# Attention and two gated MLPs on one core: weight sums made earlier, decoding tied to the hidden split, new homes for two kinds of tiles

## The chip, the core and the metric

The kernel runs on one core of a Trainium2 chip. The metric is the device time of one launch in microseconds (us), here of the only core. TensorE (PE) does the matmuls, VectorE (DVE), ScalarE (ACT) and GpSimd (POOL) the elementwise work, SyncE (SP) issues nearly all DMAs. Each engine works through its instructions in the order in which they stand in its own queue; between engines they wait on semaphores.

## What is computed

```python
scores = scale * q @ k.T              # B 4, H 8, S 576, D 64; causal window of 64
attn = softmax(where(mask, scores, -1e9)) @ v
x = attn.transpose(0, 2, 1, 3).reshape(2304, 512)
x = (sigmoid(x @ w_gate) * (x @ w_val)) @ w_out      # d_ff 1536
out = ((x @ w_a) * (x @ w_b)) @ w_out2               # d_ff 1536
```

q, k and v are 4-byte floats; the six weight matrices arrive as 8-byte floats. Every weight is taken apart on the chip into a high and a low 4-byte word (a pair), and a product of two pairs is three matmuls (high x high, high x low, low x high).

## The kernel before

**Weights.** The hidden width 1536 is cut into NF = 12 blocks of 128. Number F = 0 to 11 stands for a block of the first MLP, 12 to 23 for one of the second; each F has three matrices "a", "b", "o". `load_matrix` loads one with its 8-byte words into a tile `st` (three buffers). For the first MLP `first_words` (L378) makes the low word `low` on ACT (L382, a tile of its own with one buffer), |w| as `ex` on ACT (L385), the shifted high word `wi` on DVE (L391), and adds `low` to it on POOL (L395). `second_words` (L399) does it for the second MLP, on ACT (L404, L407, L408) and DVE (L413, L414, L416). `decode_pair` then writes the high word (ACT, L433) and the low word (DVE or POOL, L436), and the pair is stored to DRAM, to be fetched again later.

**Seven products.** Pairs of token blocks are multiplied by a scheme with seven products in place of eight. It wants sums of quarter matrices: `combining` (L450) makes four sums of matrix F on POOL (L457), their high words on ACT (L462, tiles `wq`), their low words on POOL (L465), and stores them as `kq` (L467). This is done for the second MLP alone. For the first MLP's second pass (the back blocks) `in_parts` (L864) makes the same sums from the fetched full weight `wf`: POOL L871, ACT L875, POOL L878. `weight_sums` (L318) makes the sums of the output matrices of five pairs p = 0 to 4: POOL L332 and L341 (`osum`), ACT L343 and DVE L344 (`opair`, one tile with one buffer, tag "op6"), one store of 1 MB each (L346, `ks`).

**Stages**, in order of time:
- 0 to 130 us: attention tiles and decoding of matrices F = 0 to 6, in an order written out by hand (`RAMP`).
- 130 to 270: the rest of the attention, the first MLP of the front blocks, decoding of F = 7 to 11. From here on the order is set by a scheduler that simulates a timeline.
- 270 to 343: `weight_sums` and the operands of the seven products (`front_operands`, ACT L766, DVE L772, L775), beside the last products of the first MLP (`gated` L501, `split_hidden` L490, `first_projection` L565).
- 343 to 548: twelve quads, the second MLP of the front blocks. A `quad` (L965) does the products 1, 5, 6, 2, 7, 4, 3 (`multiply`, L898); ACT copies three of them out of PSUM (`r`, L917), DVE adds them (L921, L931) and `split_hidden` splits the two halves of the hidden block (`hl` and `h`, ACT L494, DVE L496). Three PSUM banks `qa`, `qb`, `qc` are used per quad, from two pools in turn, so that product 2 of a quad, the first that writes `qc`, can only start when the quad before the last has been split out of the same bank. Behind each product `between(i)` may call `paced()` (L1224), which emits one step of decoding or of combining for a matrix two quads ahead, ordered behind the newest matmul and, on ACT, behind the newest copy `r`. Ordered here means: the scheduler must place it behind, with no semaphore.
- 548 to 572: operands for the back blocks (`operands` L800: ACT L812, DVE L813 and L820), `fetch` of matrix 0 and its `in_parts`.
- 572 to 937: both MLPs of the back blocks.

```python
            for _ in range(((0, 0, 0, 0, 2, 2, 2) if fc == 0 else (1, 1, 1, 0, 1, 1, 1))[i]):
                paced()
...
    ahead(0)
    next(unfinished[0])
    fill(len(rest))
```

The first two lines give, for each of the seven products of a quad, how many decoding steps go behind it; the last three fetch matrix 0 for the back blocks and begin its `in_parts`.

Of the kernel before, what the change touches and what calls it, by code (L numbers as in the profile page):

```python
# [23 lines left out]
def tile_window_attention_gated_mlps(ctx, tc, q, k, v, w1g, w1v, w1o, w2a, w2b, w2o, out):  # L24
# [273 lines left out]
    def whole(steps):  # L298
        while True:
            try:  # L300
                next(steps)
            except StopIteration as end:
                return end.value
# [14 lines left out]
    def weight_sums(p):  # L318

        both = late["hs"].tile([P, 2, DM], F32R, tag="hs", name="of").bitcast(F32)  # L320
        lows = {}
        for i in range(2):
            F = 2 * p + i
            if F < DECODED:
                lows[i] = late["rs"].tile([P, W], F32, tag="r", name="ol")
                for j, t in enumerate((both[:, i], lows[i])):
                    nc.sync.dma_start(out=t, in_=kept[F, "o"][:, j])
            else:
                nc.sync.dma_start(out=both[:, i], in_=kept_o[F])
        yield  # L330
        for i, low in lows.items():
            nc.gpsimd.tensor_tensor(out=both[:, i], in0=both[:, i], in1=low, op=ALU.add)  # L332
        (a11, a21), (a12, a22) = ((both[:, i, 0:CH], both[:, i, CH:]) for i in range(2))
        u, v = (late["sts"].tile([P, CH], F32, tag="s", name="osum") for _ in range(2))
        o = late["op6"].tile([P, 4, 2, CH], F32R, tag="op6", name="opair")
        for todo in (
            ((u, a21, a22, ALU.add, 0), (v, a11, a21, ALU.subtract, 2)),
            ((u, u, a11, ALU.subtract, 1), (v, a12, u, ALU.subtract, 3)),
        ):
            for s, x, y, op, _ in todo:  # L340
                nc.gpsimd.tensor_tensor(out=s, in0=x, in1=y, op=op)  # L341
            for s, _, _, _, n in todo:
                nc.scalar.activation(out=o[:, n, 0], in_=s, func=AF.Copy)  # L343
                nc.vector.tensor_tensor(out=o[:, n, 1], in0=s, in1=o[:, n, 0].bitcast(F32), op=ALU.subtract)  # L344
        yield
        nc.sync.dma_start(out=kept_sums[p], in_=o.bitcast(F32))  # L346

# [30 lines left out]
    def first_words(F, i, nm):  # L378
        st = staged.pop((F, nm))
        w0, w1 = st[:, :, 0], st[:, :, 1]  # L380
        low = dec.tile([P, DM], I32, tag="low", name="low")
        nc.scalar.activation(out=low, in_=w0.bitcast(U32), func=AF.Copy, scale=2.0 ** -29)  # L382
# [67 lines left out]
    def combining(F):  # L450
        got = parts[F]
        halves(got)
        (a1, a2), (b1, b2) = ((f[:, 0:CH], f[:, CH:]) for f in (full.pop((F, nm)) for nm in "ab"))
        sums = {}
# [9 lines left out]
        for n, (nm, t) in enumerate(tiles.items()):  # L464
            nc.gpsimd.tensor_tensor(out=t[:, 1], in0=sums[nm], in1=t[:, 0].bitcast(F32), op=ALU.subtract)  # L465
            got[nm] = (t[:, 0], t[:, 1])
            nc.sync.dma_start(out=kept_q[F - NF][:, n], in_=t.bitcast(F32))  # L467

    kept_q = [dram.tile([P, 4, 2, CH], F32, tag=f"kq{p}", name=f"kq{p}") for p in range(NF)]

# [205 lines left out]
    def step_decode(turn):  # L676

        if combined_by:
            parts_done[0] += 1
            if next(combined_by[0], combined_by) is combined_by:  # L680
                combined_by.pop()
                parts_done[0] = 0
                return True
            if parts_done[0] == 1:
                return True
# [155 lines left out]
    def fetch(F, whole):  # L841

        got = {}
        second = F >= NF
        for nm in "abo" if whole or second else "afbo":
# [4 lines left out]
            if nm == "a" and second and not whole:  # L850
                for n, k in enumerate(SUMS):
                    t = late["wq"].tile([P, 2, CH], F32R, tag="wq", name=f"wq{k}")
                    nc.sync.dma_start(out=t.bitcast(F32), in_=kept_q[F - NF][:, n])
                    got[k] = (t[:, 0], t[:, 1])
# [48 lines left out]

    nquad, copied = [0], []

    def products(ph, w, x, g, second):
# [16 lines left out]
        def finish(i, vv):  # L923
# [13 lines left out]
            else:  # L937
                t = second()
                t = (t[:, 0], t[:, 1])
            whole(split_hidden(ph, t, f))  # L940
            if second is None:
                nc.scalar.activation(out=g[i], in_=f, func=AF.Copy)
# [281 lines left out]
    def paced():  # L1224
# [5 lines left out]
        for i in nc.cur_bb.bb.instructions[since:]:  # L1230
            for after in (at, *(copied[-1:] if i.engine == mybir.EngineType.Activation else ())):
                if i.engine != mybir.EngineType.SP:
# [10 lines left out]
    for fc in range(NF):  # L1243
# [18 lines left out]
        extra = max(0, len(rest) - sum(counts[0]))  # L1262

        def between(i):
            fill(counts[0][i] + (extra if i == 4 else 0))
            for _ in range(((0, 0, 0, 0, 2, 2, 2) if fc == 0 else (1, 1, 1, 0, 1, 1, 1))[i]):
                paced()
# [48 lines left out]
    ahead(0)  # L1316
    next(unfinished[0])
    fill(len(rest))
    rest.extend(lambda j=j: half_projection(j) for j in range(2))
    held_back(lambda: next(unfinished[0]))  # L1320
    whole(unfinished.pop())
    SLOTS = {4: (1, 0, 1, 0, 1, 1, 0), 7: (0, 1, 1, 1, 2, 1, 1)}
# [143 lines left out]
```

## Time and profile before

| | us |
|---|---|
| median of 3 runs | 938.92 (937.58, 938.92, 942.02) |
| the profiled execution | 939.03 |
| its span on the core | 937.3 |
| PE busy | 919.2 (98%) |
| DVE busy | 671.7 (72%) |
| ACT busy | 506.3 (54%) |
| POOL busy | 296.9 (32%) |

The span is what the profiler saw of the core's instructions; 1.7 us of the profiled execution lie around it. PE's granted clock was 1.00 in every stretch. The chain of work that ended last lies on PE for 72% of the span, on DVE for 12%, ACT 6%, DMA 4%, POOL 4%; 2% are issue. An engine's idle time counts only where PE waits behind it.

### The profile page before, as it was taken

The numbers are of one execution on the slowest core, as the hardware profiler recorded it, in microseconds if no ns is written. First come the engines' busy times: TensorE is split into PE (matmuls) and PEld (weight loads), VectorE is DVE, ScalarE is ACT, GpSimd is POOL, SyncE is SP. The second block draws the span as 40 slices with busy tenths as digits, with TensorE's granted clock in tenths as the row PEclk, the third lists the DMA queues.
The fourth block names the chain that finished last, engine by engine and source line by source line (L and its number), as shares of the span: only waits on it lengthen the run. The fifth ranks groups of instructions, "written<-read, shape, count | busy, mean of one in ns | idle before, by whom it ended". The sixth has DMA issues, their size and how long they took to land.

```text
span 937.3 us, 15579 instructions
## 1 busy us (share of the span) xinstructions
PE 919.2 (98%) x5498; PEld 772.3 (82%) x5498; DVE 671.7 (72%) x1334; ACT 506.3 (54%) x1107; POOL 296.9 (32%) x325
## 2 busy tenths in 40 slices
PE   7899999999999999999999999999999999999998
PEld 6798888887888787888887887888888888888886
DVE  6997787785756778778888776688877773354455
ACT  7897555676754548785686445654544333211211
POOL 4543222332326723361653348345341000000000
PEclk9999999999999999999999999999999999999999
DMA  8988597985676824864966768454547574555212
GB/s 216 262 217 227 197 333 282 338 285 167 213 257 252 299 113 141 283 223 185 336 234 216 266 173 239 176 180 168 180 148 241 176 278 146 169 157 151 85 57 90
DMA packets 145564, 195.78 MB, mean 209 GB/s; under 512 B 63568, under 2 KB 98640, under 8 KB 144848
## 3 DMA queue, kind: packets, MB, share of 16 engines
q1 hardware_dynamic: 144400, 192.71, 62.6%
q0 software_dynamic: 1088, 2.10, 1.4%
q8 instruction: 43, 0.70, 0.3%
q14 instruction: 33, 0.27, 0.1%
HBM read 118.75 MB, written 71.57 MB: 203 GB/s over the span
## 4 chain that ended last, share of the span: by engine, by line
PE 72%; DVE 12%; ACT 6%; DMA 4%; POOL 4%; issue 2%; SPq 0%; DVEq 0%; POOLq 0%; ACTq 0%
PE qa L898 17%; PE accq L1037 12%; PE qb L898 8%; PE gps L485 7%; PE vps L485 6%; PE accm L587 6%; PE qc L898 4%; PE accy L1000 3%; PE accx L1000 2%; PE xps L231 2%; PE sps L173 1%; POOL s L457 1%; PE tps L221 1%; DMA st_b<-in_moe_w_b_dram 1%; PE acc L538 1%
## 5 line engine op out<-in xcount | busy, mean ns | idle before, releaser
L898 PE MATMUL qa<-op,wq 128*128 128x512 f32 x432 | 112.5, 390 | 1.0 <-ACT r L917 1.0
L917 ACT ACTIVATE r<-qa 128x512 f32<-128x512 f32 x108 | 62.7, 595 | 92.2 <-PE qa L898 90.9
L898 PE MATMUL qb<-op,wq 128*128 128x512 f32 x432 | 110.4, 389 | 0.0
L485 PE MATMUL vps<-xh,wb 128*128 128x256 f32 (+1 forms) x392 | 104.9, 337 | 0.8 <-ACT hr L505 0.8
L485 PE MATMUL gps<-xh,wa 128*128 128x256 f32 (+1 forms) x392 | 104.5, 337 | 0.0
L898 PEld LDWEIGHTS qa<-op,wq 128*128 128x128 f32 x432 | 81.0, 188 | 18.2 <-ACT r L917 1.4
L898 PEld LDWEIGHTS qb<-op,wq 128*128 128x128 f32 x432 | 81.1, 188 | 17.1 <-ACT op L766 0.2
L395 POOL TENSOR_TENSOR wi<-wi,low 128x512 int32<-128x512 int32 x36 | 49.4, 1373 | 127.6 <-DVE wi L391 80.6
L587 PE MATMUL accm<-hh,wo 128*128 128x512 f32 (+1 forms) x296 | 84.9, 356 | 0.4 <-ACT hh L494 0.4
L485 PEld LDWEIGHTS vps<-xh,wb 128*128 128x128 f32 x392 | 68.7, 189 | 8.7 <-ACT hr L505 1.0
L485 PEld LDWEIGHTS gps<-xh,wa 128*128 128x128 f32 x392 | 68.7, 189 | 8.2 <-DVE hl L496 0.4
L1037 PE MATMUL accq<-wo,h 128*128 128x512 f32 (+1 forms) x294 | 71.0, 385 | 0.1
L494 ACT ACTIVATE hh<-qa 128x512 fp32r<-128x512 f32 x36 | 21.4, 596 | 88.6 <-DVE qa L931 55.4
L485 PE MATMUL gps<-xl,wa 128*128 128x256 f32 (+1 forms) x196 | 65.9, 336 | 0.6 <-DVE xl L240 0.6
L485 PE MATMUL vps<-xl,wb 128*128 128x256 f32 (+1 forms) x196 | 65.7, 335 | 0.0
L1037 PEld LDWEIGHTS accq<-wo,h 128*128 128x128 f32 x294 | 54.5, 188 | 11.3 <-DVE res L1041 0.3
L878 POOL TENSOR_TENSOR wq<-s,wq 128x256 fp32r<-128x256 f32 x48 | 38.4, 868 | 76.0 <-ACT wq L875 76.0
L587 PEld LDWEIGHTS accm<-hh,wo 128*128 128x128 f32 x296 | 52.9, 189 | 9.2 <-ACT hh L494 0.6
L898 PE MATMUL qc<-op,wa 128*128 128x512 f32 x216 | 56.7, 390 | 2.4 <-DVE h L496 2.4
L192 ACT ACTIVATE pr<-pr,stat 128x128 f32<-128x128 f32 x144 | 54.1, 392 | 4.2 <-DVE stat L186 4.0
L898 PE MATMUL qa<-op,wa 128*128 128x512 f32 x216 | 56.0, 390 | 0.2 <-DVE g L921 0.2
L1037 PE MATMUL accq<-wo,hh 128*128 128x512 f32 x184 | 55.1, 391 | 0.2
(198 smaller groups left out, 2160.1 us busy)
## 6 DMA issues: line engine op xcount, KB each, us to landing
wo<-ko SPq DMA_DIRECT2D x27, 512.0 KB, 4.2
wa<-ka SPq DMA_DIRECT2D x27, 512.0 KB, 4.3
st_o<-in_moe_w_out_dram SPq DMA_DIRECT2D x24, 512.0 KB, 5.8
ka<-wa SPq DMA_DIRECT2D x24, 512.0 KB, 5.4
kb<-wb SPq DMA_DIRECT2D x24, 512.0 KB, 5.7
ko<-wo SPq DMA_DIRECT2D x24, 512.0 KB, 5.1
kq<-wq SPq DMA_DIRECT2D x48, 256.0 KB, 5.0
wq<-kq SPq DMA_DIRECT2D x48, 256.0 KB, 3.1
```

Of the source, the lines that this page charges most:

```text
L173: nc.tensor.matmul(sps[e][rows, j, :], lhsT=qt[dims, j, rows], rhs=kt[dims, j, s * WIN:s * WIN + P], start=True, stop=True,)
L192: nc.scalar.activation(out=pr[e][:, j, :], in_=pr[e][:, j, :], func=AF.Exp, bias=nmax[:, e, j:j + 1], scale=-1.0, accum_out=None if t in O ...
L231: nc.tensor.matmul(xps[dims, j, rows], lhsT=vv[:, 2 * j + e, :], rhs=pt[e][:, j, rows], start=True, stop=True)
L395: (nc.vector if F >= NF else nc.gpsimd).tensor_tensor(out=wi, in0=wi, in1=low, op=ALU.add)
L485: nc.tensor.matmul(ps, lhsT=a[:, c * P:(c + 1) * P], rhs=b[:, c, :], start=(n == 0), stop=(n == 3 * NP - 1))
L494: nc.scalar.activation(out=hh, in_=hr, func=AF.Copy, scale=factor)
L587: nc.tensor.matmul(ps[:, m], lhsT=a[:, sl], rhs=b, start=k == 0, stop=k == total - 1)
L878: nc.gpsimd.tensor_tensor(out=t[:, 1], in0=sums[nm], in1=t[:, 0].bitcast(F32), op=ALU.subtract)
L898: nc.tensor.matmul(ps, lhsT=a[:, c * P:(c + 1) * P], rhs=b[:, c, :], start=first and n == 0, stop=n == 5, skip_group_check=True,)
L917: nc.scalar.activation(out=r[n], in_=ps, func=AF.Copy)
L1000: nc.tensor.matmul(bank[k], lhsT=a[n][i][:, sl], rhs=b[n][j], start=start and m == 0, stop=m == 2, skip_group_check=True,)
L1037: nc.tensor.matmul(ps, lhsT=a, rhs=b, start=n == 0, stop=n == len(pairs) - 1)
```

## The change

Five things are done.

1. `weight_sums`: for p = 3 the four parts of `opair` go to tiles of `quarter(1, 0)` and `quarter(1, 1)` (one buffer each; every call makes a tile), not to the "op6" tile. All five stores are cut into four of 256 KB.
2. `first_words`: from F = 7 on, `low` is written over the low words in the loaded tile itself, in steps of 8 bytes.
3. `combining` also makes the sums of F = 0, out of the kept full weight, which it loads into an `st` tile (`st_f`); it does so beside the last quad. `fetch` then loads these four sums from `kq`, and the `in_parts` of matrix 0 goes. That of matrices 1 and up stays.
4. The decoding step behind the second product of a quad goes behind the fourth (products 5 and 2).
5. `paced` also orders its DVE instructions behind the newest split `hl` of a hidden block.

```diff
@@ weight_sums
-        o = late["op6"].tile([P, 4, 2, CH], F32R, tag="op6", name="opair")
+        if p == 3:
+            o = [quarter(1, i, "opair").rearrange("p a (b c) -> p a b c", b=2)[:, j] for i in range(2) for j in range(2)]
+        else:
+            o = late["op6"].tile([P, 4, 2, CH], F32R, tag="op6", name="opair")
+            o = [o[:, n] for n in range(4)]
...
-                nc.scalar.activation(out=o[:, n, 0], in_=s, func=AF.Copy)
-                nc.vector.tensor_tensor(out=o[:, n, 1], in0=s, in1=o[:, n, 0].bitcast(F32), op=ALU.subtract)
-        yield
-        nc.sync.dma_start(out=kept_sums[p], in_=o.bitcast(F32))
+                nc.scalar.activation(out=o[n][:, 0], in_=s, func=AF.Copy)
+                nc.vector.tensor_tensor(out=o[n][:, 1], in0=s, in1=o[n][:, 0].bitcast(F32), op=ALU.subtract)
+        yield
+        for n in range(4):
+            nc.sync.dma_start(out=kept_sums[p][:, n], in_=o[n].bitcast(F32))
@@ first_words
-        low = dec.tile([P, DM], I32, tag="low", name="low")
+        low = w0 if F >= DECODED else dec.tile([P, DM], I32, tag="low", name="low")
@@ combining
-        got = parts[F]
-        halves(got)
-        (a1, a2), (b1, b2) = ((f[:, 0:CH], f[:, CH:]) for f in (full.pop((F, nm)) for nm in "ab"))
+        got = parts.get(F, {})
+        if F >= NF:
+            halves(got)
+            whole_ones = [full.pop((F, nm)) for nm in "ab"]
+        else:
+            f = stage.tile([P, DM, 2], I32, tag="st", name="st_f").bitcast(F32).rearrange("p f t -> p (f t)")
+            whole_ones = [f[:, 0:DM], f[:, DM:]]
+            nc.sync.dma_start(out=f.rearrange("p (i f) -> p i f", i=2), in_=kept[F, "f"])
+            yield
+        (a1, a2), (b1, b2) = ((f[:, 0:CH], f[:, CH:]) for f in whole_ones)
...
+    MADE = 1
@@ fetch
-        second = F >= NF
+        second = F >= NF or F < MADE
@@ products.finish
             whole(split_hidden(ph, t, f))
+            for made, names in zip(nc.cur_bb.bb.instructions[-2:], halves_made):
+                names.append(made.name)
@@ paced
-            for after in (at, *(copied[-1:] if i.engine == mybir.EngineType.Activation else ())):
+            newest = {mybir.EngineType.Activation: copied[-1:], mybir.EngineType.DVE: halves_made[1][-1:]}
+            for after in (at, *newest.get(i.engine, ())):
@@ the quads
+        if fc == NF - 1:
+            combined_by.extend(combining(F) for F in reversed(range(MADE)))
...
-            for _ in range(((0, 0, 0, 0, 2, 2, 2) if fc == 0 else (1, 1, 1, 0, 1, 1, 1))[i]):
+            for _ in range(((0, 0, 0, 0, 2, 2, 2) if fc == 0 else (1, 0, 1, 1, 1, 1, 1))[i]):
@@ back blocks
     ahead(0)
-    next(unfinished[0])
     fill(len(rest))
     rest.extend(lambda j=j: half_projection(j) for j in range(2))
-    held_back(lambda: next(unfinished[0]))
-    whole(unfinished.pop())
```

Lines further down move: L343 becomes L347, L413, L414, L416 become L418, L419, L421, L496 becomes L509, L505 becomes L518, L917 becomes L930.

The change also moves instructions, since the scheduler orders anew. Two places matter below. The first is ACT's queue at the end of the first MLP, about 328 us, where the sums for p = 3 are made: `opair` are ACT's high words of these sums, `hr` and `hh` the hidden block's steps that PE waits for, `op2` an operand. Before:

```order
L343 ACTIVATE opair_4528<-osum_4526 128x256
L343 ACTIVATE opair_4528<-osum_4527 128x256
L505 ACTIVATE hr_4571<-gps_4545 128x512
L343 ACTIVATE opair_4528<-osum_4526 128x256
L766 ACTIVATE op2_4598<-gacc31_2077 128x1024
L343 ACTIVATE opair_4528<-osum_4527 128x256
L505 ACTIVATE hr_4627<-gps_4601 128x256
L494 ACTIVATE hh_4574<-vps_4558 128x512
```

And now:

```order
L518 ACTIVATE hr_4572<-gps_4546 128x512
L347 ACTIVATE opair10_4523<-osum_4521 128x256
L347 ACTIVATE opair11_4525<-osum_4522 128x256
L779 ACTIVATE op2_4602<-gacc31_2078 128x1024
L347 ACTIVATE opair10_4524<-osum_4521 128x256
L347 ACTIVATE opair11_4526<-osum_4522 128x256
L518 ACTIVATE hr_4631<-gps_4605 128x256
L507 ACTIVATE hh_4575<-vps_4559 128x512
```

The 512-wide `hr` now stands ahead of all four `opair`. The tiles `opair10_4523` and `opair10_4524` share the one buffer of `quarter(1, 0)`, as `opair11_4525` and `opair11_4526` share that of `quarter(1, 1)`.

The second place is DVE's queue in the quads, about 490 us, where the eighth quad's hidden block is finished: `ex` are decoding steps, `qc` the finished second half of the block in its PSUM bank, `h1` its split, which frees the bank. Before:

```order
L921 TENSOR_TENSOR g0_6244<-qc_6248,r1_6255 128x512
L931 TENSOR_TENSOR qc_6117<-qc_6117,g1_6114 128x512
L413 TENSOR_SCALAR ex_6259<-ex_6259 128x512
L413 TENSOR_SCALAR ex_6287<-ex_6287 128x512
L414 TENSOR_SCALAR ex_6259<-ex_6259 128x512
L414 TENSOR_SCALAR ex_6287<-ex_6287 128x512
L416 ISA ex_6259<-ex_6259,low_6257 128x1024
L496 SCALAR_TENSOR_TENSOR h1_6241<-qc_6117,h1_6241 128x512
```

And now:

```order
L944 TENSOR_TENSOR qc_6121<-qc_6121,g1_6118 128x512
L441 TENSOR_TENSOR wb_6168<-ex_6160,wb_6168 128x512
L421 ISA ex_6206<-ex_6206,low_6204 128x1024
L934 TENSOR_TENSOR g0_6248<-qc_6252,r1_6259 128x512
L509 SCALAR_TENSOR_TENSOR h1_6245<-qc_6121,h1_6245 128x512
L418 TENSOR_SCALAR ex_6307<-ex_6307 128x512
L419 TENSOR_SCALAR ex_6307<-ex_6307 128x512
L418 TENSOR_SCALAR ex_6263<-ex_6263 128x512
```

Between the finished half and its split five decoding steps stood before; now two others and an addition stand there, and the long row of decoding steps follows the split.

## Rows read from the trace of the kernel before

**Rows 1.** Windows by stage: length, busy time (instructions) of each engine, clock, DMA.
```profile
0.00:20.00 20.00, 14.68 (x187) 12.01 (x188) 12.56 (x70) 13.91 (x44) 9.35 (x21) 1.00 0.89 217
...
130.00:270.00 140.00, 139.24 (x1122) 117.90 (x1121) 100.06 (x254) 88.24 (x227) 42.20 (x33) 1.00 0.77 253
270.00:343.00 73.00, 71.80 (x360) 60.36 (x359) 50.65 (x82) 37.39 (x74) 41.85 (x45) 1.00 0.70 256
343.00:548.00 205.00, 202.15 (x970) 169.18 (x970) 165.11 (x259) 138.69 (x254) 81.68 (x90) 1.00 0.64 226
548.00:572.00 24.00, 23.04 (x126) 19.75 (x125) 19.83 (x17) 14.28 (x29) 18.95 (x18) 1.00 0.90 225
...
732.00:937.30 205.30, 201.68 (x923) 167.79 (x922) 104.35 (x153) 49.12 (x82) 0.00 (x0) 1.00 0.44 142
sum 937.30, PE 919.25 PEld 772.33 DVE 671.73 ACT 506.35 POOL 296.90; mean PE 91.92 PEld 77.23 DVE 67.17 ACT 50.63 POOL 29.69
```

**Rows 2.** Waits of PE from 130 us on: total us, times, longest us.
```profile
PE qc L898 <- DVE h L496: 2.4, 2, 1.6
PE qa L898 <- ACT r L917: 1.0, 1, 1.0
PE vps L485 <- ACT hr L505: 0.8, 1, 0.8
PE xps L231 <- ACT pt L121: 0.8, 1, 0.8
PE accm L587 <- ACT hh L494: 0.4, 1, 0.4
PE qa L898 <- DVE g L921: 0.2, 1, 0.2
```

**Rows 3.** Timeline about 215 us, POOL and ACT: start, us, engine, line, operation.
```profile
214.60 1.30 POOL L395 TENSOR_TENSOR wi<-wi,low 128x512 int32<-128x512 int32 x1 [1.15 <-DVE wi L391]
...
215.93 0.69 ACT L382 ACTIVATE low<-st_o 128x512 int32<-128x512 uint32 x1 [1.89 <-POOL wi L395]
```

**Rows 4.** Groups of instructions: line, engine, operation, count; busy, mean ns; idle before.
```profile
L395 POOL TENSOR_TENSOR wi<-wi,low 128x512 int32<-128x512 int32 x36 | 49.4, 1373 | 127.6 <-DVE wi L391 80.6
...
L404 ACT ACTIVATE low<-st_a 128x512 uint16<-128x512 uint32 x12 | 9.5, 788 | 6.1 <-DVE ex L416 6.1
```

**Rows 5.** Timeline about 328 us: POOL, ACT, PE.
```profile
326.99 2.29 POOL L341 TENSOR_TENSOR osum<-of 128x256 f32<-128x256 f32 x2
...
328.71 0.42 ACT L343 ACTIVATE opair<-osum 128x256 fp32r<-128x256 f32 x1 [2.73 <-DMA ks<-opair]
...
329.64 0.58 ACT L505 ACTIVATE hr<-gps 128x512 f32<-128x512 f32 x1
...
332.58 0.36 ACT L505 ACTIVATE hr<-gps 128x256 f32<-128x256 f32 x1
...
333.88 0.28 PE L485 MATMUL gps<-xh,wa 128*128 128x256 f32 x1
```

**Rows 6.** All instructions with the tensors kq: their DMAs.
```profile
DMA to landing us min/median/max: 2.4/3.9/6.3
```

**Rows 7.** Timeline of DVE in the quads, about 490 us.
```profile
490.24 1.35 DVE L413 TENSOR_SCALAR ex<-ex 128x512 f32<-128x512 f32 x2
...
491.51 1.85 DVE L414 TENSOR_SCALAR ex<-ex 128x512 int32<-128x512 int32 x2
...
493.88 0.68 DVE L496 SCALAR_TENSOR_TENSOR h<-qc,h 128x512 fp32r<-128x512 f32 x1
```

**Rows 8.** Timeline before the back blocks, about 560 us: DVE, POOL, ACT.
```profile
551.99 1.22 DVE L820 TENSOR_TENSOR t<-xq,t 128x1024 f32<-128x1024 f32 x1
...
561.50 5.32 DVE L820 TENSOR_TENSOR t<-xq,t 128x1024 f32<-128x1024 f32 x1
...
561.74 3.29 POOL L878 TENSOR_TENSOR wq<-s,wq 128x256 fp32r<-128x256 f32 x4
...
566.85 1.06 ACT L812 ACTIVATE op<-t 128x1024 fp32r<-128x1024 f32 x1 [2.73 <-DVE t L820]
```

More of the change, by code (lines that the diff above doesn't have):

```diff
@@ L466, in combining @@
             got[nm] = (t[:, 0], t[:, 1])
-            nc.sync.dma_start(out=kept_q[F - NF][:, n], in_=t.bitcast(F32))
-    kept_q = [dram.tile([P, 4, 2, CH], F32, tag=f"kq{p}", name=f"kq{p}") for p in range(NF)]
+            nc.sync.dma_start(out=kept_q[F][:, n], in_=t.bitcast(F32))
+    MADE = 1
+    kept_q = {F: dram.tile([P, 4, 2, CH], F32, tag=f"kq{F}", name=f"kq{F}") for F in (*range(MADE), *range(NF, 2 * NF))}
     def halves(got):
@@ L679, in step_decode @@
             parts_done[0] += 1
-            if next(combined_by[0], combined_by) is combined_by:
+            if next(combined_by[-1], combined_by) is combined_by:
                 combined_by.pop()
@@ L852, in fetch @@
                     t = late["wq"].tile([P, 2, CH], F32R, tag="wq", name=f"wq{k}")
-                    nc.sync.dma_start(out=t.bitcast(F32), in_=kept_q[F - NF][:, n])
+                    nc.sync.dma_start(out=t.bitcast(F32), in_=kept_q[F][:, n])
                     got[k] = (t[:, 0], t[:, 1])
@@ L902, in multiply @@
                 n += 1
-    nquad, copied = [0], []
+    nquad, copied, halves_made = [0], [], ([], [])
     def products(ph, w, x, g, second):
```

## The prediction

> **What bounds the kernel now.** I read the windows by stage first [rows 1]. PE is busy for 919.25 of the 937.30 us of the span at a granted clock of 1.00, so 18.05 us are idle. Of these, 5.32 lie in the first 20 us, and 8.66 in all before 130 us (18.05 less the rest, which follows). The change leaves the hand-written order there as it is. In the last stretch 3.62 are idle, which is the end after PE's last matmul: the change does not touch it either. What remains is 0.76 at 130 to 270 us, 1.20 at 270 to 343, 2.85 in the quads (343 to 548) and 0.96 at 548 to 572: 5.77 us. The list of PE's waits from 130 us on names nearly all of it: 2.4 + 1.0 + 0.8 + 0.8 + 0.4 + 0.2 = 5.6 us [rows 2]. The reader should see two things. DVE is busy for 165 of 205 us in the quads and ACT for 139, so a faster or lighter helper is worth nothing by itself; only those seven waits can be won. And PE's count of matmuls is the same in the new program, so that the new time is the old one, less the waits that go, plus the waits that come. The ceiling of the gain is 5.6 us, or 0.6% of 938.92. A measurement of this kernel can tell about 0.5% from no change, which is 4.7 us: the change would have to remove five sixths of all waits, and add none, to be seen as faster.
>
> I now price the change by stage, since each wait belongs to one edit.
>
> **Low words in place (130 to 270 us).** The one wait here is PE's 0.8 for ACT's `pt` [rows 2]. Ahead of `pt` on ACT stands a `low` that waited 1.89 us for POOL's `wi`, which was still reading the one `low` buffer [rows 3]. In place, `low` needs no buffer, and this wait of ACT has no cause left. Costs: ACT now writes its 15 `low` (5 matrices of 3) in steps of 8 bytes. The dense write took 0.69 [rows 3], a write that skips every second half word 0.79 [rows 4]; 15 x 0.10 = 1.5 us of ACT at most, beside 88 of 140 busy, hidden by ACT's idle time. POOL reads with the same step; no row shows such a read, and its dense price is 1.37 [rows 4]. I bound it by that and by half as much again (0.7 us more, an estimate, a third of the 1.89 that ACT waited): ACT no longer waits for it. The loaded tile is held until POOL has read it, some 3 us longer per load; there are three of them, and each matrix's load has a whole turn of some 28 us (140 us for 5 matrices). The order of attention and products is shuffled anew from about 130 us on, so that a wait of the same length can come elsewhere. Between -0.8 and +0.8 I take **-0.4**, half of the wait: its cause goes, its place does not stay.
>
> **Second home for the sums of p = 3 (270 to 343 us).** Before, ACT waited 2.73 for the 1 MB store of p = 2 at 328.71, and `hr` stood behind two `opair`, so it came at 329.64 and PE waited 0.8 for it [rows 2, 5]. In the new order this `hr` stands ahead of the four `opair`: the 0.8 goes. But a new wait comes. Each call of `quarter(1, 0)` makes a tile, and the tag has one buffer, so the second tile (`opair10_4524`) waits until the store of the first has landed, and the same for `quarter(1, 1)`. Behind these two `opair` on ACT stand the 256-wide `hr` and then `hh`, which PE needs. The sums of POOL end at 326.99 + 2.29 = 329.28 [rows 5]; one `opair` of 0.42 and its low word of about as much bring the store to 330.1, and it lands 2.4 to 6.3 us later, 3.9 in the middle of stores and loads of that size [rows 6]. Then `opair` 0.42 and `hr` 0.36 [rows 5]: `hr` is there at 333.3, 334.8 or 337.2. PE wants it for the `gps` that began at 333.88 [rows 5], or at 333.05 once the 0.8 is gone: a wait of 0.25, 1.75 or 4.15. The 0.4 for `hh` [rows 2] that came behind is taken up in it. In sum -1.2 + 0.25 = -0.95, +0.55 or +2.95. The middle row mixes the whole kernel. At 328.71 the queue held little else, and ACT's wait for a store four times as large was 2.73 [rows 5]; I take 3.0 us to landing, so **-0.4**, and keep -1.0 and +2.9 for the range.
>
> The Trainium skill speaks against the cutting of the stores: its page "DMA: Bandwidth & Descriptors", section "Anatomy of one DMA — SWDGE (gpsimd) path", gives every DMA some 2.0 us of its own, mostly the receipt of the last write, and 436 GB/s beyond it. By that a 256 KB store takes 2.6 us (estimate) and not a quarter of the 1 MB store's time, and this term would be -0.75. The page fitted it for another kind of queue, and no run here separates the receipt; the shortest landing of that size, 2.4 [rows 6], is near it.
>
> SP issues 15 more stores. Nothing that PE needs stands close behind them there: the loads behind are for matrices two quads ahead.
>
> **Tied decoding and the moved step (343 to 548 us).** PE waited 2.4 in two places for DVE's split `h`, the longest 1.6, and 0.2 for an addition [rows 2]. The cause stands in DVE's queue: in front of the split at 493.88 lie two decoding steps at 490.24 (1.35) and two at 491.51 (1.85) [rows 7], 3.2 us of work that no one needed soon. In the new order the split stands ahead of such a row, at this place and at the other. So 2.6 go. In exchange decoding finishes later, and ACT, which works in order, has copies `r` for PE behind `wq` and `wa` that wait for DVE and POOL. The matrices have time, two quads; the copies `r` have not. I count one new wait of the size of the smaller of today's two, 2.4 - 1.6 = 0.8, since the order shows one or two places where an `r` comes that close. **-1.8**; between -2.6 (none) and +1.6 (both stay, one more of 1.6). The step moved from the second to the fourth product is part of the same order and not priced again.
>
> **Sums of matrix 0 made earlier (548 to 572 us).** PE waited 1.0 for ACT's `r` [rows 2]. Behind it: DVE's `t` at 561.50 took 5.32, where the same instruction took 1.22 at 551.99; beside it ran POOL's four `wq` sums, 3.29 in all, from 561.74; ACT waited 2.73 for `t`, and `r` stood behind [rows 8]. These four, and the four before them, go. They now lie beside the last quad: POOL is busy for 82 of 205 us in the quads [rows 1], so eight more of some 0.8 us (3.29 for four [rows 8]) find room, and their stores and the loads have the whole stretch of 24 us behind the quads to land, ahead of the products that want them. The sums of matrix 1 stay, and come earlier than before, since their load moves up by one. If they fall beside `t`, it takes 1.22 + 3.29 = 4.5 and not 5.32: 0.8 of the 1.0 is won all the same. Between -0.8 and -1.0: **-0.9**. If all eight of POOL's instructions for matrix 1 fell beside it, 0.
>
> By the Trainium skill, page "SBUF — State Buffer", section "Who interferes with whom", a DVE instruction with two SBUF inputs and a POOL instruction that reads SBUF lock each other out for whole instructions. By that rule the change only wins as far as POOL is silent during `t`; the row agrees, with POOL at its usual pace and `t` 4.1 us longer.
>
> **Sum.** -0.4 - 0.4 - 1.8 - 0.9 = -3.5. Against the profiled execution (939.03, 1.7 us more than its span and 0.1 above the median of 938.92) this is **935.5 us**, or 0.4% faster: within what counts as no change.
>
> **The rivals.**
> - *The waits only move* (0.27). The scheduler sets the order by a model of its own; each wait that goes is replaced by one of like size, as the 0.8 of the `opair` place shows in small. For it: every gain here rests on a new order; the wait of the second `quarter` tile is real. Against it: at three of the four places the cause itself is gone. Time: 939.0 less the 0.9 of the sums, plus up to 2.9 of the `quarter` tiles: 937.5 to 941, at 939.0 in the middle.
> - *All waits go* (0.13). The new store lands in 2.4 us, no copy `r` is late: 939.0 - 5.6 = 933.4. For it: the order as it stands. Against: 5.6 is everything.
> - *Slower: ACT becomes late in the quads* (0.08). Decoding's DVE steps are now held behind the split of the quad, so ACT's `wa`, `wb` and POOL's sums of that matrix come later, and the `r` or `hh` behind them on ACT in turn; PE waits for it at product 7 or at the next quad. Price: as long as today's longest, 1.6 us, in half of the quads would be 6 x 1.6 = 9.6, less the 2.6 and the 1.7 of the other terms, so 944.3 (939.0 + 9.6 - 2.6 - 1.7); in every quad 953.9. It decides when those 3.2 us of decoding, put off, reach past the slack of an `r`. Against it: ACT is idle for 66 of 205 us there [rows 1].
>
> **How the numbers follow.** The forecast has 0.52 (934.2 to 937.5), the rivals 0.27, 0.13 and 0.08. Faster by over 0.5% means below 934.2: 0.13 of all waits gone and 0.02 of the forecast's lower end, 0.15. Slower by over 0.5% means above 943.6: 0.08. The rest, 0.77, is the same. For the range I leave out the slower rival (0.08), the lowest of the case in which all goes (0.05) and the highest of the moved waits (0.04): 932.9, half a us below the ceiling for the spread of the runs, to 941.0.
>
> **What would show it.** Right: no wait of PE for `h` in the quads; DVE's `t` near 561 us at 1.2 to 4.5 us; the first 512-wide `hr` ahead of all `opair`; ACT's wait for a `ks` store now at the second `quarter` tile, with a PE wait for the `gps` behind it of 0.2 to 1.8 us; total idle of PE from 130 to 572 us at 2 to 3 us in place of 5.8. Wrong: PE waits for `r` in several quads, or for `hr` by 3 us and more; a wait for `wq` at the first product of the back blocks; a stretch from 130 to 270 us with more than 1.6 idle.

## The result, and the profile after

The changed kernel takes 945.75 us (median of 6 runs, 944.77 to 947.62), against 939.05 for the kernel before (6 runs, 937.58 to 942.02). The ratio is 1.0069 [1.0054, 1.0084]: 6.7 us slower. The forecast of 935.5 has the wrong sign, and 945.75 lies above its range.

The profiled execution of after took 944.77 us, with a span of 943.0: 5.7 us more than before [rows 1]. Its windows by stage (columns as in [rows 1]):

```profile
130.00:270.00 140.00, 137.51 (x1072) 115.92 (x1072) 97.06 (x251) 87.72 (x226) 40.69 (x32) 0.99 0.75 244
270.00:343.00 73.00, 69.86 (x377) 58.43 (x377) 48.31 (x78) 36.67 (x71) 40.10 (x44) 1.00 0.78 270
343.00:548.00 205.00, 200.90 (x965) 167.83 (x964) 165.42 (x260) 138.70 (x259) 88.05 (x100) 1.00 0.65 229
548.00:572.00 24.00, 24.00 (x141) 21.29 (x140) 18.78 (x22) 12.36 (x21) 6.75 (x7) 1.00 0.87 245
```

PE's idle time from 130 to 572 us is 2.49 + 3.14 + 4.10 + 0 = 9.73 us, where before had 5.77 and the forecast wanted 2 to 3. The stretch from 130 to 270 has 2.49 idle and a clock of 0.99, so the sign "more than 1.6" of the prediction came true. The stretch from 548 to 572 is full, as forecast. PE's waits from 130 us on (columns as in [rows 2]):

```profile
PE xps L231 <- ACT pt L121: 2.5, 1, 2.5
PE gps L498 <- ACT hr L518: 1.8, 1, 1.8
PE accm L600 <- DVE gacc L576: 1.7, 2, 1.2
PE accq L1052 <- DVE resf L1056: 1.6, 1, 1.6
PE qa L911 <- ACT r L930: 1.4, 1, 1.4
PE accq L1052 <- ACT hh L507: 0.5, 1, 0.5
```

They add up to 9.5 us against 5.6. All seven waits of before are gone, and seven new ones stand elsewhere. That holds for `pt` too. The wait of before lay near 217 us (first line below). In after, PE does not idle at all from 130 to 246 us (second line); its wait of 2.5 for `pt` lies near 250 us and has another cause.

```profile
217.64 0.34 PE L231 MATMUL xps<-pt,vb 128*64 128x64 f32 x4 [0.76 <-ACT pt L121]
130.00:246.00 116.00, 116.00 (x883) 97.53 (x882) 86.47 (x218) 74.61 (x192) 37.29 (x29) 1.00 0.84 272
```

**The hand-over to the second MLP, about 248 us.** The timeline of after, ACT, then PE, then SP's queue (start, us, engine, line, operation, idle time before and its releaser):

```profile
245.75 0.58 ACT L518 ACTIVATE hr<-gps 128x512 f32<-128x512 f32 x1
248.70 0.78 ACT L409 ACTIVATE low<-st_a 128x512 uint16<-128x512 uint32 x1 [2.37 <-DMA st_a<-in_moe_w_a_dram]
...
250.06 0.56 ACT L121 ACTIVATE pt<-tps 128x512 f32<-128x512 f32 x1
...
250.68 0.47 PE L231 MATMUL xps<-pt,vb 128*64 128x64 f32 x4 [2.49 <-ACT pt L121]
...
244.76 0.38 SPq L361 DMA_DIRECT2D st_a<-in_moe_w_a_dram  x1
```

ACT stands still for 2.37 us on `low` of matrix 12 "a", the first of the second MLP, whose load was issued at 244.76 and has not landed. The `pt` that PE needs stands behind it. ACT's queue in the two programs shows that this is new. Before, `pt` stands right behind `hr`. The two steps of matrix 12 (`low` of `st_a`, L404 and L408) follow much later, behind the `hr` and `hh` of other blocks:

```
L505 ACTIVATE hr_3634<-gps_3608 128x512
L121 ACTIVATE pt15_1_3560<-tps15_1_3555 128x512
...
L505 ACTIVATE hr_3854<-gps_3828 128x256
L494 ACTIVATE hh_3857<-vps_3841 128x256
L404 ACTIVATE low_4211<-st_a_4025 128x512
L408 ACTIVATE low_4211<-st_a_4025,start_91 128x512
```

And in the changed program:

```
L518 ACTIVATE hr_3626<-gps_3600 128x512
L409 ACTIVATE low_4200<-st_a_4013 128x512
L413 ACTIVATE low_4200<-st_a_4013,start_91 128x512
L121 ACTIVATE pt15_1_3552<-tps15_1_3547 128x512
```

The trace of before has `pt` at 246.14 us and matrix 12's first step only at 268.18, right behind POOL's last addition for the first MLP, which reads the one `low` buffer until 268.14:

```profile
266.54 1.60 POOL L395 TENSOR_TENSOR wi<-wi,low 128x512 int32<-128x512 int32 x1 [12.26 <-DVE wi L391]
268.18 0.79 ACT L404 ACTIVATE low<-st_a 128x512 uint16<-128x512 uint32 x1
```

So the freed buffer let this step move some 20 us ahead, to where its load had not landed.

**The sums for p = 3, about 335 us.** The timeline of after for ACT, PE and POOL:

```profile
331.35 0.57 ACT L518 ACTIVATE hr<-gps 128x512 f32<-128x512 f32 x1
...
337.56 1.06 ACT L779 ACTIVATE op<-gacc 128x1024 fp32r<-128x1024 f32 x1 [1.56 <-DVE gacc L576]
338.52 0.40 ACT L347 ACTIVATE opair<-osum 128x256 fp32r<-128x256 f32 x1
339.64 0.42 ACT L347 ACTIVATE opair<-osum 128x256 fp32r<-128x256 f32 x1 [0.72 <-DMA ks<-opair]
339.97 0.37 ACT L518 ACTIVATE hr<-gps 128x256 f32<-128x256 f32 x1
...
340.39 0.39 PE L498 MATMUL gps<-xh,wa 128*128 128x256 f32 x1 [1.84 <-ACT hr L518]
...
337.07 0.74 POOL L345 TENSOR_TENSOR osum<-of,osum 128x256 f32<-128x256 f32 x1 [0.42 <-DVE opair L348]
```

The 512-wide `hr` runs ahead of the `opair` of p = 3, and PE does not wait for it. The 256-wide `hr` comes behind the second `quarter` tile, and PE waits 1.84 us. Only 0.72 of that is ACT's wait for the store, though. Ahead of both stands `op`, which waited 1.56 us for DVE's `gacc` and then took 1.06. POOL had ended the last sum for p = 3 at 337.81, before ACT came to it.

**The quads.** The timeline of after, ACT and PE about 478 us:

```profile
476.24 0.66 ACT L412 ACTIVATE ex<-st_a 128x512 f32<-128x512 f32 x1 [2.86 <-POOL s L469]
476.80 1.32 ACT L474 ACTIVATE wq<-s 128x256 fp32r<-128x256 f32 x4
478.03 0.77 ACT L409 ACTIVATE low<-st_o 128x512 uint16<-128x512 uint32 x1
478.67 0.64 ACT L412 ACTIVATE ex<-st_o 128x512 f32<-128x512 f32 x1
479.22 0.85 ACT L413 ACTIVATE low<-st_o,start 128x512 f16<-128x512 f32 x1
479.94 0.57 ACT L507 ACTIVATE hh<-qa 128x512 fp32r<-128x512 f32 x1
480.41 0.59 ACT L930 ACTIVATE r<-qa 128x512 f32<-128x512 f32 x1
...
481.05 1.43 PE L911 MATMUL qa<-op,wq 128*128 128x512 f32 x5 [1.43 <-ACT r L930]
```

ACT waits 2.86 us for POOL's sums and then works off five groups of decoding and combining before it reaches `hh` and `r`. Their times add up to 4.24 us (0.66 + 1.32 + 0.77 + 0.64 + 0.85); since they overlap a little, `hh` starts 3.70 us after the first. The same row of steps stands on ACT from 509.36 on. This time DVE is behind too. DVE and PE of after about 513 us:

```profile
512.55 0.97 DVE L418 TENSOR_SCALAR ex<-ex 128x512 f32<-128x512 f32 x1 [2.21 <-POOL wq L477]
513.44 0.68 DVE L1056 TENSOR_TENSOR resf<-accq,resf 128x512 f32<-128x512 f32 x1
...
514.17 1.65 PE L1052 MATMUL accq<-wo,h 128*128 128x512 f32 x6 [1.55 <-DVE resf L1056]
```

**Stage by stage.** The next table takes the starts of single instructions: the ramp ends with DVE's 200th instruction, the quads run from PE's first `qa` to the first 256-wide `gps` of the back blocks, which is followed by the stretch to the first `accx` of the back blocks. The ramp itself takes 55.4 to 57.6 us from one execution to the next, whatever the kernel, and is left out; what follows, to the end of PE's last matmul, takes 344.4 to 344.5 in all kernels.

| kernel | ramp to quads | quads | to the back's first accx |
|---|---|---|---|
| before | 286.22 | 203.38 | 44.43 |
| after | 292.31 | 204.00 | 43.17 |
| after_again (the same program) | 291.57 | 204.03 | 43.17 |
| in_place_only | 292.18 | 203.47 | 44.44 |
| own_low | 287.74 | 203.97 | 43.17 |
| in_place_but_last | 286.48 | 204.01 | 43.17 |
| order_later | 288.54 | 203.96 | 43.17 |
| sums_only | 287.29 | 203.39 | 44.44 |
| one_tile | 292.50 | 203.93 | 43.17 |
| untied | 292.27 | 203.40 | 43.19 |
| but_last_untied | 286.43 | 202.58 | 43.19 |
| made_only | 285.64 | 204.23 | 43.17 |
| made_and_counts | 285.69 | 202.95 | 43.19 |
| made_counts_low_but_last | 285.70 | 203.71 | 43.19 |

The loss sits before the quads: +6.1, then +0.6 in them, -1.3 behind them. Each row is one execution. The two of the changed program differ by 0.74 in the first column and by 0.03 in the second, so a difference of less than some 0.7 in the first column tells nothing.

### The profile page after: what moved, and what is told of

It reads as the page before. It is cut to its first block, busy times and chain, and to the rows that moved or that the text cites. A ratio compares the mean times of both kernels' runs of the same rounds, so it can differ in the third digit from the quotient of the medians.

```text
span 943.0 us, 15669 instructions
## 1 busy us (share of the span) xinstructions
PE 921.8 (98%) x5498; PEld 774.6 (82%) x5498; DVE 667.6 (71%) x1334; ACT 506.3 (54%) x1107; POOL 289.5 (31%) x325
## 4 chain that ended last, share of the span: by engine, by line
PE 75%; DVE 9%; ACT 6%; DMA 4%; POOL 4%; issue 2%; SPq 0%; POOLq 0%; DVEq 0%; ACTq 0%
PE qa L911 17%; PE accq L1052 12%; PE qb L911 8%; PE gps L498 7%; PE vps L498 7%; PE accm L600 6%; PE qc L911 4%; PE accy L1015 3%; PE accx L1015 2%; PE xps L231 2%; PE sps L173 2%; PE tps L221 1%; DVE ex L421 1%; POOL osum L345 1%; DVE ex L418 1%
## 5 line engine op out<-in xcount | busy, mean ns | idle before, releaser
L930 ACT ACTIVATE r<-qa 128x512 f32<-128x512 f32 x108 | 62.7, 594 | 95.9 <-PE qa L911 94.7
L891 POOL TENSOR_TENSOR wq<-s,wq 128x256 fp32r<-128x256 f32 x44 | 34.9, 813 | 78.6 <-ACT wq L888 78.6
L911 PE MATMUL qa<-op,wb 128*128 128x512 f32 x216 | 55.1, 390 | 0.0
```

Of the source, the lines that this page charges most:

```text
L911: nc.tensor.matmul(ps, lhsT=a[:, c * P:(c + 1) * P], rhs=b[:, c, :], start=first and n == 0, stop=n == 5, skip_group_check=True,)
L930: nc.scalar.activation(out=r[n], in_=ps, func=AF.Copy)
```

## The experiments

Three sets of four kernels ran, each set beside the kernel before on one chip (its medians there: 938.91, 939.08, 939.21). Before the first set the theory was that the loaded tile is held longer, so that the load of matrix 12 comes late (theory 1); its rivals were the new order as such (theory 2), the `quarter` tiles and the tied decoding. Theory 3 came behind the first set: low words in place take away the wait that kept matrix 12's first steps behind `pt` on ACT.

**Which part it is: own_low, in_place_only.** The first takes low words in place out of the change (first set), the second puts them alone into the kernel before (third set).

```diff
@@ own_low, against after
-        low = w0 if F >= DECODED else dec.tile([P, DM], I32, tag="low", name="low")
+        low = dec.tile([P, DM], I32, tag="low", name="low")
@@ in_place_only, against before
-        low = dec.tile([P, DM], I32, tag="low", name="low")
+        low = w0 if F >= DECODED else dec.tile([P, DM], I32, tag="low", name="low")
```

> The change with its low words in a tile of their own again. If the loaded tile, held until POOL has read it, is what makes the load of the first matrix of the second MLP late (theory 1), ACT's wait for that load (2.4 us), PE's wait of 2.5 for pt behind it and the fall of the clock behind that (0.91 granted at 250 to 270 us, 1.8 us) go: 941 to 942.5 us, and 1.00 granted there. If the new order as such brought the wait (theory 2), a wait of 1.5 us and more stays there: 944 to 946.

> The kernel before with the low words in place and nothing else. Theory 3 (its order has the first step of matrix 12 ahead of pt on ACT, as in the change): the 5.8 us that the change loses before the first quad come from this part alone, with 2.5 of them as a wait for pt near 250 us: 943.5 to 945.5 us. If the five parts must come together for the loss: 938.5 to 941.

own_low: 941.11 us (12 runs), ratio 1.0018 [1.0005, 1.0030]. in_place_only: 945.0 (6 runs), 1.0054 [1.0033, 1.0075]. One line by itself brings most of the loss: +6.0 in the first column of the table. Its waits of PE from 130 us on:

```profile
PE accm L587 <- DVE gacc L563: 3.2, 1, 3.2
...
PE xps L231 <- ACT pt L121: 2.4, 1, 2.4
```

The 2.4 for `pt` is the one of after; the 3.2 for `gacc`, near 312 us, is new too. The traces show a way to it. SP's queue, first in in_place_only, then in before:

```profile
276.61 0.38 SPq L356 DMA_DIRECT2D st_b<-in_moe_w_b_dram  x1
277.04 1.45 SPq L327 DMA_DIRECT2D ol<-ko  x3
...
271.39 1.91 SPq L327 DMA_DIRECT2D ol<-ko  x3
274.51 0.38 SPq L356 DMA_DIRECT2D st_b<-in_moe_w_b_dram  x1
```

The load of `st_b`, of the second MLP, now stands ahead of the loads `ol` that `weight_sums` begins with. SP waits 3.0 us there for ACT's `low`, and POOL's first addition for the sums begins at 283.57 in place of 277.63. Followed back from PE's wait for `gacc`, the chain runs over DVE's decoding steps and ACT to these sums of POOL's. SP has the new order in after and order_later as well, the old one in own_low and in_place_but_last. No run changes the order of these loads alone, so this second price of the line is read from traces and not shown by a run.

**Is it the place in ACT's queue: in_place_but_last, order_later.** The first keeps the shared `low` buffer for the last matrices of the first MLP (F = 11) only, so that matrix 12's `low` must wait for POOL to have read it. The second leaves all low words in place and orders ACT's first instructions of matrix 12 "a" behind POOL's last addition of F = 11, without a semaphore.

```diff
@@ in_place_but_last, against after
-        low = w0 if F >= DECODED else dec.tile([P, DM], I32, tag="low", name="low")
+        low = w0 if DECODED <= F < NF - 1 else dec.tile([P, DM], I32, tag="low", name="low")
@@ order_later, against after
         (nc.vector if F >= NF else nc.gpsimd).tensor_tensor(out=wi, in0=wi, in1=low, op=ALU.add)
+        last_add.append(nc.cur_bb.bb.instructions[-1].name)
...
+            since = len(nc.cur_bb.bb.instructions)
             whole(decode_words(*m))
+            if F == NF and nm == "a":
+                for made in nc.cur_bb.bb.instructions[since:]:
+                    if made.engine == mybir.EngineType.Activation:
+                        tc.add_manual_dep(
+                            made, last_add[-1],
+                            mybir.DependencyInfo(mybir.DependencyClass.NoSync, mybir.DependencyReason.DATA), reason="later"
+                        )
```

> The change, with the low words in place for F = 7 to 10, but not for F = 11, whose tile the load of matrix 12 takes over. Theory 1 (the tile held too long at the hand-over to the second MLP): as with all of them in their own tile, 941 to 942.5. If the writes and reads in steps of 8 bytes are what costs: 944.5 to 946, since 12 of 15 stay.

> The change with all 15 low words in place; only ACT's first two instructions for matrix 12 are ordered behind POOL's last addition for matrix 11, which puts them behind pt in ACT's queue. If the place in the queue is the cause (theory 3: without the wait for the one low buffer the scheduler put the first step of matrix 12, whose load has not landed, ahead of pt), the wait for pt goes as fully as with F = 11 in its own tile: 939.5 to 941 us. If the tile that is held longer is the cause (theory 1), decoding of matrix 12 is as late as before and the waits behind it stay: 943 to 945.

in_place_but_last: 940.21 (12 runs), 1.0012 [1.0003, 1.0021]. order_later: 940.89 (12 runs), 1.0022 [1.0013, 1.0031]; **after_again**, the changed kernel once more in the same set, 944.92 (5 runs), 1.0057 [1.0045, 1.0069].

> The changed kernel itself once more, on the same chip as the three beside it. 945 to 946.5 us, with PE's wait of 2.5 for pt near 250 us; the granted clock of each run tells how often the clock falls behind that wait (0.996 or 0.998 of the span) and what such a run costs against one at 1.000: some 2 us.

With one order on ACT added, 4.0 of the 5.8 us come back (944.92 less 940.89; before took 939.08). in_place_but_last fits theory 1 as well as theory 3, so it is order_later that parts them. after_again came out just below its 945 to 946.5, and none of its runs had a mean clock of 1.000 to compare with. The timeline of ACT in order_later:

```profile
245.55 0.58 ACT L519 ACTIVATE hr<-gps 128x512 f32<-128x512 f32 x1
246.03 0.59 ACT L121 ACTIVATE pt<-tps 128x512 f32<-128x512 f32 x1
```

`pt` runs at 246.03, where after has it at 250.06. The tile that is held longer is not enough by itself: order_later holds it too, and issues the load of matrix 12 as late as after does (244.66 and 244.76 us; before 243.66), yet PE does not wait. What order_later keeps of the loss (its first column is 2.3 above before) are waits of 2.2 for `gacc` and 1.8 for `hr`, both in other places.

**The second home: sums_only, one_tile.** sums_only puts the first part of the change alone into the kernel before (third set); one_tile leaves the change as it is, but asks for each quarter tile once, so that no second tile waits for the first one's store (first set).

```diff
@@ one_tile, against after
-            o = [quarter(1, i, "opair").rearrange("p a (b c) -> p a b c", b=2)[:, j] for i in range(2) for j in range(2)]
+            o = [quarter(1, i, "opair").rearrange("p a (b c) -> p a b c", b=2) for i in range(2)]
+            o = [t[:, j] for t in o for j in range(2)]
```

> The kernel before with the second home for the sums of p = 3 and the stores cut in four, and nothing else. By my forecast's term -0.4 (between -1.0 and +2.9): 938.5 us. If the second tile of a quarter waits for the first one's store and hr for PE stands behind it, a wait of 0.7 to 1.9 for hr or hh near 335 us stays: 939 to 940.5. If a home of its own for p = 3 is worth what it was meant for, both waits (0.8 and 0.4) go: 937.7.

> The change, with one tile per quarter for the sums of p = 3 in place of two that share a buffer. If the wait of the second tile for the first one's store is the cause of PE's wait of 1.84 for hr at 340 us, that wait goes: 943.5 to 944.5 us. If the sums themselves are late (POOL's osum behind a load), hr stays late by 1 us and more: 945 to 946.5.

sums_only: 939.89 (12 runs), 1.0000 [0.9986, 1.0014], so its runs don't tell it from before; in its profile the stage before the quads is 1.1 us longer, since waits of `accm` for `hh` (1.3) and `gacc` (1.2) stand where 0.8 and 0.4 stood. one_tile: 945.51 (6 runs), 1.0067 [1.0052, 1.0083], a miss for the theory that the wait for the store costs what PE waits there. Its waits of PE:

```profile
PE accm L601 <- DVE gacc L577: 3.5, 2, 2.1
...
PE accm L601 <- ACT hh L508: 0.7, 1, 0.7
PE gps L499 <- ACT hr L519: 0.7, 1, 0.7
```

`hr` fell from 1.8 to 0.7, and `gacc` and `hh` took it back.

**The tie: untied, but_last_untied.** Both leave out the order of DVE's decoding behind the newest split `hl`; the second has in_place_but_last's line as well.

```diff
@@ paced, against after
-            newest = {mybir.EngineType.Activation: copied[-1:], mybir.EngineType.DVE: halves_made[1][-1:]}
+            newest = {mybir.EngineType.Activation: copied[-1:]}
```

> The change without the order of decoding's DVE steps behind the hidden split. If the tie brought the three new waits in the quads (r 1.43, resf 1.55, hh 0.5), they go and the two for h (2.4) come back: 944 to 945.5 us. If the moved step (second to fourth product) brought them, they stay and those for h come on top: 946 to 948.5.

> As the change with F = 11 in its own low tile (940.2), and without the order of decoding's DVE steps behind the hidden split. If the tie brought the three waits in the quads (3.5 in all), and the two for h (2.4) come back: 939.0 to 939.8 us. If the quads' waits come of the moved step: 940 to 941.

untied: 943.13 (6 runs), 1.0042 [1.0028, 1.0055]. The waits of 1.43 and 1.55 at the two places shown are gone, others of 1.4 (for `g`), 0.9 (`r`) and 0.8 (`h`) come, and the quads take 203.40 as before. Its time lies below both expected ranges: 2.6 us below the 945.75 of the change, where the quads are only 0.6 shorter. Where the rest comes from isn't shown. but_last_untied: 938.82 (11 runs), 0.9993 [0.9983, 1.0004], just below its range of 939.0 to 939.8. Without the tie and without the hand-over's fault the loss is gone, and nothing is won.

**What pays: made_only, made_and_counts, made_counts_low_but_last.** The kernel before with the sums of matrix 0 made early (second set); with the moved decoding step too (third set); and with low words in place for F = 7 to 10 on top (third set). All three are untied.

```diff
@@ made_and_counts, against made_only
-            for _ in range(((0, 0, 0, 0, 2, 2, 2) if fc == 0 else (1, 1, 1, 0, 1, 1, 1))[i]):
+            for _ in range(((0, 0, 0, 0, 2, 2, 2) if fc == 0 else (1, 0, 1, 1, 1, 1, 1))[i]):
@@ made_counts_low_but_last, against made_and_counts
-        low = dec.tile([P, DM], I32, tag="low", name="low")
+        low = w0 if DECODED <= F < NF - 1 else dec.tile([P, DM], I32, tag="low", name="low")
```

> The kernel before with one part of the change alone, the sums of matrix 0 made beside the last quad. The wait of 1.0 for r near 569 us goes, and with it 1.0 to 1.3 us: 937.5 to 938.2. If the new stores and sums in the last quads bring a wait of their own: 938.5 to 940.

> The kernel before with the sums of matrix 0 made beside the last quad and the decoding step moved from the second to the fourth product, and nothing else. If the moved step is what changes the waits for h in the quads (2.5 in the run without it), they shrink or go: 935.8 to 937.3 us. If the moved step does nothing: 938.1, as without it. If it brings waits of its own: 939 and more.

> The same, with the low words in place for F = 7 to 10 besides: the change without its two losing parts (F = 11 in place, the tie) and without the second home for the sums. If low words in place are worth PE's wait of 0.8 for pt at 217 us and nothing else: 0.8 below the kernel without them beside it. If the order before the first quad gets worse with them: above it.

made_only: 938.09 (11 runs), 0.9988 [0.9979, 0.9997]. made_and_counts: 937.40 (12 runs), 0.9980 [0.9966, 0.9994]. made_counts_low_but_last: 937.35 (12 runs), 0.9979 [0.9965, 0.9992]. made_and_counts, with two of the five parts, ends 0.1 above its expected range and 1.8 us below the kernel before. That is under the 0.5% at which I called a kernel changed, but its interval excludes 1. Its largest waits of PE:

```profile
PE gps L493 <- DVE g L929: 1.4, 1, 1.4
PE xps L231 <- ACT pt L121: 1.0, 1, 1.0
PE qc L906 <- DVE h L504: 0.9, 1, 0.9
```

Of the two waits for `h`, the one of 1.6 is gone without any tie: the moved step alone does that. Low words in place for four matrices take the wait for `pt` away as well, and waits of 1.4 (`hr`) and 0.6 (`r`) come in its stead; the time stays (937.35), 0.8 less was expected.

## Why the prediction was wrong

**Low words in place: forecast -0.4, measured +4.6 in its stage** (after less own_low; alone +6.0). This is the step that failed. What the term saw was right: the wait of 0.8 for `pt` near 217 us is gone with the low words in place, and is still there, 0.76, in own_low. The term asked whether a cause of ACT's wait goes, how much longer the strided write takes and how long the tile is held, and bounded what might come by "a wait of the same length". It did not ask what else the one `low` buffer did: it also held matrix 12's `low` behind POOL's last addition, and so `pt` ahead of it on ACT. With the buffer free, the scheduler put that step ahead of `pt`; on the chip ACT stood still for 2.37 us before the load had landed. (That the scheduler's own timeline has the load land sooner is likely, and wasn't tested.) The row was there to be read: ACT's new queue about 248 us shows a first touch of a freshly loaded tile between `hr` and `pt`. The prediction read the new order at two other places and settled this one by a bound of its old size. The loads' new order in SP's queue, above, is a second thing that it did not look for: it said of SP's queue only that the loads behind the new stores are not needed soon.

The new waits do not make up the whole 6.1 us of the stage. From 130 us to the quads PE waits 6.0 us in after (2.5 + 1.8 + 1.7) against 2.0 (0.8 + 0.8 + 0.4), which is +4.0; a fall of the clock behind the gap adds 1.7 (below). In in_place_only the 6.0 us are made up otherwise: waits of 5.6 (3.2 + 2.4), and the clock fell behind the other gap.

**Second home: forecast -0.4, measured +1.1** (sums_only's profile, same stage; its runs' ratio is 1.0000). The mechanism was right to the row: the first `hr` ahead of the sums, the wait now at the second `quarter` tile, PE waiting 1.84 where 0.25, 1.75 or 4.15 stood. The 256 KB stores landed in 2.9 us (median of the ten from 325 to 345 us; 2.3 to 4.4), where 3.0 was taken. The estimate of 2.6 by the Trainium skill's "DMA: Bandwidth & Descriptors", section "Anatomy of one DMA — SWDGE (gpsimd) path", lies between the shortest and the median. What failed was the belief that the store ends last there: PE's wait was 1.84, the store's share 0.72 behind an `op` that the sum did not have, and one_tile gained nothing without it.

**Tied decoding and the moved step: forecast -1.8, measured +0.6.** The 2.6 of `h` and `g` went, as said. But three waits came, 1.4 + 1.6 + 0.5 = 3.5, where one of 0.8 was priced. They look like what the slower rival named, ACT late behind put-off decoding, in two or three of twelve quads and not in half. But untied has the same row on ACT near that place, with a wait of 2.91 for POOL's sums: there `hh` stands ahead of four of the five groups, `r` comes at 479.41, and PE, which had waited 2.6 us earlier in the quads, comes late enough not to wait for it. So that the tie makes ACT late is not shown; that it costs is: 0.6 in the quads (after less untied) and 1.4 (in_place_but_last less but_last_untied). The price of 0.8 came from the size of an old wait and not from the queue, where ACT's five groups between POOL's sums and `r`, 4.24 us of work, were to be read. And one edit did the work of two: "not priced again" hid that the moved step alone takes away the 1.6 and shortens the quads by 1.3 (made_and_counts less made_only).

**Sums of matrix 0: forecast -0.9, measured -1.3 in its stage** in every kernel that has them, and -1.0 us in made_only. The stretch is without a wait. DVE's `t` that took 5.32 [rows 8] takes 1.23 now (L833, at 570.07), with POOL busy for 6.75 of the 24 us in place of 18.95; the slow addition is now the one before it, and PE does not wait for it:

```profile
566.98 3.05 DVE L826 TENSOR_TENSOR op<-t,op 128x1024 fp32r<-128x1024 f32 x1
570.07 1.23 DVE L833 TENSOR_TENSOR t<-xq,t 128x1024 f32<-128x1024 f32 x1
```

That the -1.0 of made_only equals the old wait is in part luck: its quads, where the sums now lie, take 0.85 longer (204.23 against 203.38), which the term had at nothing, and its first column is 0.6 shorter, which two runs of one program can differ by.

The sum by steps: 4.6 + 1.1 + 0.6 - 1.3 = 5.0, of 5.7 between the two spans; the ramp took 0.5 more in this execution of after (55.95 and 55.45). The 0.6 of the quads in it is of three edits, since the sums of matrix 0 lie there too. The sentence that PE's count of matmuls is the same held (5498 in both traces). The rival "the waits only move" had the right idea and the wrong bound: a moved wait need not keep its size.

## What to carry to other kernels

A buffer with one slot is also a rule of order: before removing it, look up what else waited for it, and read the new queue of each in-order engine for a first touch of freshly loaded data that now stands ahead of work on the path. Price a new wait by the work queued between the late input and the copy that PE needs, not by the size of an old wait. Read the queue of the engine that issues the DMAs in the same way. Try the parts of a joint change one by one: here two of five carried all of the gain and one line most of the loss.

## What was not expected of the hardware

The windows of after behind the 2.49 us gap (columns as above; the clock is the third number from the end):

```profile
250.00:252.00 2.00, 1.32 (x25) 1.33 (x27) 0.00 (x0) 2.00 (x10) 0.00 (x0) 0.68 0.03 8
252.00:254.00 2.00, 2.00 (x20) 1.88 (x18) 0.58 (x4) 2.00 (x11) 1.04 (x1) 0.50 0.19 45
254.00:256.00 2.00, 2.00 (x18) 2.00 (x18) 0.81 (x2) 1.54 (x5) 1.04 (x1) 0.97 0.68 179
```

The granted clock fell from 1.00 to 0.50, that is from 2.4 to 1.2 GHz, about when PE came back from the gap, and was up again by about 254 us. That cost 2 x (0.32 + 0.50 + 0.03) = 1.7 us. It doesn't fall each time. after_again, the same program, has the same gap of 2.5 us and a clock of 1.00 behind it; so have the profiles of in_place_only and one_tile (2.4 and 2.6 us, 1.00 from 250 to 270 us). In after_again and in_place_only it fell behind PE's wait for `gacc` instead, of 1.9 and 3.2 us. after_again behind the gap near 250 us, then in_place_only behind its wait for `gacc`:

```profile
250.00:256.00 6.00, 5.50 (x66) 5.30 (x67) 1.99 (x7) 5.76 (x23) 2.08 (x2) 1.00 0.33 87
312.00:316.00 4.00, 4.00 (x10) 3.13 (x11) 3.30 (x5) 2.99 (x5) 0.43 (x1) 0.50 0.66 248
```

So the gap near 250 us cost 2.5 us in one execution of the program and 2.5 + 1.7 = 4.2 in another. What decides between the two is open. The times point the same way: one_tile's three runs with a mean clock of 1.000 took 944.06 to 944.64 us, its three at 0.996 to 0.998 took 946.37 to 946.87. Only the profiled one of them has a trace, so where the clock fell in the others isn't shown; in after it was low in the first 20 us too (0.91, where before has 1.00).
